# A decay table with the head innermost, and its rows from a second set of powers

## The chip, the cores and the metric

The kernel runs on one NeuronCore of one Trainium2 chip. Five engines work beside each other: TensorE (PE, with its weight loads as PEld), VectorE (DVE), ScalarE (ACT), GpSimd (POOL) and SyncE (SP), which only issues DMAs. The metric is the time of one execution in microseconds (us), as the median of several runs. Before the change it is 601.41 us, the median of 3 runs from 600.75 to 603.45.

## What is computed

Three layers follow each other. The first is retention attention over 2 batches, 8 heads, 768 positions and 64 columns per head, with one decay factor per head:

```
Dmask = where(i >= j, lam[h] ** (i - j), 0)            # within a block
intra = ((q @ k.T) * Dmask) @ v
inter = (q * lam[h] ** (i + 1)) @ kv_state             # from the blocks before
out   = intra + inter
kv_state = lam[h] ** block * kv_state + (k * lam[h] ** (block - 1 - j)).T @ v
```

Its output, 1536 tokens by 512, goes through `relu(x @ w_in)**2 @ w_out` (2048 hidden columns) and then through `(sigmoid(x @ w_gate) * (x @ w_val)) @ w_out` (1536 hidden columns). All is float32. The decay factors `lam` are an input, so the tables of their powers are made on the chip.

## The kernel before

The attention works in chunks of 128 positions (CH), so there are 12 chunks, 6 for each batch, taken in the order ORDER. Two tables hold the decay. `D` is [128, 8, 128]: for each key position j (the partition; keys lie in reverse order), head h and query position i, it holds lam to the power that the pair needs, or zero. `L` is [128, 4, 128]: lam to the power i + 1 for the head to which the partition belongs.

`powers()` (L203) makes them. It loads `lam` into `lam_sb`, POOL raises it to powers 1 to 128 (`W`, L217), and ACT's queue stores 127 zeros, a one and these powers as one row of 256 numbers per head in DRAM (`w_dram`, L216 and L219). `decays()` (L223) reads them back: for D each partition starts one element further on in every head's row, so it reads eight pieces of 512 bytes, one for each head. L is read in pieces of 512 bytes too, four per partition (L231).

A chunk takes these steps. `att_scores` (L258) is q times k on PE, with two heads side by side. `att_prep` (L269) has POOL make `kd`, which is k times the last column of D (L278), and `qd`, q times L (L285), while DVE makes `at`, scores times D (L287), in two instructions per chunk, one for the even heads and one for the odd. `att_decay` (L293) is `tt` on POOL, `att_out` (L301) the products with v and with the state, `att_state` and `att_x` the evacuations. POOL does nothing after the attention.

The first 7 chunks (LEAD) are a prologue. It starts with the loads: FIRST and SIDE name q/k and k/v loads that precede D and L, EARLY (L28) those that follow: "D v1 w q4" is the two tables, the second k/v, a weight and the fifth q/k. The q's of SIDE go through ACT's queue, all others through SP's. The 5 other chunks lie in the first 16 steps of the first layer (`step_1`), which PE fills with matrix products. Beside them ACT and DVE turn weights into the form that PE uses: DVE's `m`, `u` and `wlo` (L172 to L167, L374) belong to that. Each engine works through its instructions in the order in which the program issues them; nothing overtakes.

After the 16 steps, `strassen` computes the rest of the first layer with fewer products (`block`, L545, after `combine_x` and `combine_a`), then come `pair_out` (L695) and the second layer in the same three stages.

Of the kernel before, what the change touches and what calls it, by code (L numbers as in the profile page):

```python
# [7 lines left out]
F32 = mybir.dt.float32  # L8
F32R = mybir.dt.float32r
AF = mybir.ActivationFunctionType  # L10
ALU = mybir.AluOpType

P = 128
CH = 128
# [10 lines left out]

FIRST = "q0 q1 v0"
SIDE = "q2 q3"
EARLY = "D v1 w q4"  # L28
LOOP = ("v2 v3 q5", "q6 v4 v5 w", "v6 w v7", "q7", "", "", "")
RAW_BUFS = 4  # L30

# [9 lines left out]
def retention_moe_kernel(  # L41
# [24 lines left out]
    nc = tc.nc  # L66
# [3 lines left out]
    H = lam.shape[0]  # L70
    NF1 = w1.shape[0]
    NF2 = w2.shape[0]
    I32 = mybir.dt.int32

    const = ctx.enter_context(tc.tile_pool(name="const", bufs=1))
    dram = ctx.enter_context(tc.tile_pool(name="dram", bufs=1, space=bass.MemoryType.DRAM))
# [5 lines left out]
    def bank():  # L82
        return ps.tile([P, 512], F32, tag="p", name="p")

    def unit(name, dt=F32):
        return up.tile([P, 512], dt, tag="u", name=name)

    def double(name, dt=F32):
        return wp.tile([P, 2, 512], dt, tag="w", name=name)
# [21 lines left out]
    def load_qk(c, eng=nc.sync):  # L111
        qk_t[c] = double("qk")
        eng.dma_start(out=qk_t[c], in_=qk[c].rearrange("a t p b -> a t (p b)"))

    def load_kv(c, eng=nc.sync):
        kv_t[c] = double("kv")
        eng.dma_start(out=kv_t[c], in_=kv[c].rearrange("s t h d -> s t (h d)"))
# [12 lines left out]
    def load_w(n):  # L130
        for _ in range(min(n, len(to_load))):
            ph, f, u = key = to_load.pop(0)
            t = wp.tile([P, 512, 2], I32, tag="w", name="raw")
            src = (w1 if ph == 1 else w2)[f, u].bitcast(I32)
            nc.sync.dma_start(out=t, in_=src.rearrange("p (n two) -> p n two", two=2))
            raw_t[key] = t
# [51 lines left out]
    def run(ops):  # L188
        weave(ops, [])


    lam_sb = const.tile([P, 1], F32, name="lam_sb")
    exi = const.tile([P, 8], I32, name="exi")
    ex = const.tile([P, 8], F32, name="ex")
    W = const.tile([P, 8], F32, name="W")
    Z = const.tile([H, 128], F32, name="Z")
    warm = const.tile([P, P], mybir.dt.bfloat16, name="warm")
    D = const.tile([P, H, CH], F32, name="D")
    L = const.tile([P, 4, CH], F32, name="L")
    S = [const.tile([P, 4, 64], F32, name=f"S{i}", tag=f"S{i}") for i in range(2)]  # L200
    w_dram = dram.tile([H, 256], F32, name="w_dram")

    def powers():  # L203


        src = bass.AP(lam.tensor, lam.offset, [[1, H], [0, 16], [1, 1]])
        nc.sync.dma_start(out=lam_sb, in_=src)
        nc.vector.memset(warm, 0.0)
        nc.gpsimd.iota(exi, pattern=[[1, 8]], base=0, channel_multiplier=8)
        nc.vector.memset(Z[:, 0:127], 0.0)  # L210
        nc.vector.memset(Z[:, 127:128], 1.0)
        nc.vector.tensor_scalar(
            out=exi, in0=exi, scalar1=127, scalar2=None, op0=ALU.bitwise_and
        )
        nc.vector.tensor_scalar(out=ex, in0=exi, scalar1=1.0, scalar2=None, op0=ALU.add)
        nc.scalar.dma_start(out=w_dram[:, 0:128], in_=Z)  # L216
        nc.gpsimd.tensor_tensor(out=W, in0=lam_sb.to_broadcast([P, 8]), in1=ex, op=ALU.pow)  # L217
        dst = w_dram[:]
        nc.scalar.dma_start(  # L219
            out=bass.AP(dst.tensor, dst.offset + 128, [[256, H], [8, 16], [1, 8]]), in_=W  # L220
        )

    def decays():  # L223


        src = w_dram[:]
        nc.sync.dma_start(
            out=D, in_=bass.AP(src.tensor, src.offset, [[1, P], [256, H], [1, CH]])
        )
        for r in range(2):  # L230
            nc.sync.dma_start(  # L231
                out=L[64 * r : 64 * r + 64],
                in_=bass.AP(src.tensor, src.offset + 256 * r + 128, [[0, 64], [512, 4], [1, CH]]),
            )

    def warm_up():

        t = bank()
        for _ in range(WARM):
            nc.tensor.matmul(t[:, 0:P], lhsT=warm, rhs=warm, start=True, stop=True)  # L240

    Dv = D.rearrange("j (p r) i -> j r p i", r=2)

# [9 lines left out]
    def pv(t):  # L255
        return t.rearrange("a (p b) -> a p b", p=4)
# [12 lines left out]
    def att_prep(c):  # L269
        n = c % SEQ_CH  # L270
        sc = sc_t.pop(c)
        at_t[c] = double("at")
        dst = [pv(at_t[c][:, r, :]) for r in range(2)]
        qt = qk_t.pop(c)[:, 0, :]
        kn = kv_t[c][:, 0, :]
        if n < SEQ_CH - 1:
            kd = kd_t[c] = unit("kd")
            nc.gpsimd.tensor_tensor(  # L278
                out=kd.rearrange("s (h d) -> s h d", h=H),
                in0=kn.rearrange("s (h d) -> s h d", h=H),  # L280
                in1=D[:, :, CH - 1 : CH].to_broadcast([P, H, 64]), op=ALU.mult,
            )
        if n > 0:
            qd = qd_t[c] = unit("qd")
            nc.gpsimd.tensor_tensor(out=pv(qd), in0=pv(qt), in1=L, op=ALU.mult)  # L285
        return [
            lambda r=r: nc.vector.tensor_tensor(  # L287
                out=dst[r], in0=pv(sc[r]), in1=Dv[:, r], op=ALU.mult
            )
            for r in range(2)  # L290
        ]
# [431 lines left out]
    def load(what, eng=nc.sync):  # L723

        for x in what.split():
            if x == "w":
                load_w(1)
            elif x == "D":
                decays()
            elif x[0] == "q":  # L730
                load_qk(order[int(x[1:])], eng)
            else:
                load_kv(order[int(x[1:])], eng)
# [4 lines left out]
    for k in range(lead, NCH):  # L738
        a, b = SLOTS[k - lead]
# [64 lines left out]

    with tc.manual_schedule():
        powers()
        load(FIRST)
        load(SIDE, nc.scalar)
        warm_up()
        load(EARLY)  # L810
        new_xr()
        for k in range(UP):
            att_scores(order[k])
        run(att_prep(order[0]))
        for k, c in enumerate(order[:lead]):
            att_out(c)
            if UP <= k + 3 < lead:
                att_scores(order[k + 3])
            load(LOOP[k])
            ops = conv_dve()  # L820
            if k + 1 < lead:
                weave(att_prep(order[k + 1]), ops[:2])
                run(att_state(c))
                att_decay(order[k + 1])
                weave(ops[2:], att_x(c))
            else:
                weave(split_w(1, 0), ops)
                rest.append(c)
            for m in range(CONVS[k]):
                if m:  # L830
                    run(conv_dve())
                conv_act()
            flush()


        keys = [(1, i, 0) for i in range(NF1 // 2)]
        prepare_a(keys[0], T1)
        at(T1 - 20.0, lambda: load_a((1, 1, 0)))
        combine_x([T1 + d for d in (-30, -25, -15, -13, -11, -9, -7, 2, 4, 6, 8)])
        for f in range(NF1):  # L840
            step_1(f)
        n_out = 24
        for k in range(n_out):
            convert(T2 + 1.0 + k * (T3 - T2 - 4.0) / n_out)
        for f in range(NF1):
            prepare_out(1, f, T2 + 24 * MM * f)
        uses = [use for i in range(NF1 // 2) for use in pair_in_1(i)]
        strassen(keys, uses, (None, lambda: close(1)))
        xc.clear()
        new_xr()  # L850
        for f in range(2):
            at(T3 - 24.0 + f, lambda f=f: load_units(2, f))
        at(T3 - 14.0, lambda: run(split_w(2, 0)))
        pair_out(1)


        for f in range(2, NF2):
            at(T3 + (36 * (f - 1) - 12) * MM - 8.0, lambda f=f: load_units(2, f))
        for k in range(3 * NF2 - n_out):
            convert(T3 + 2.0 + 3.6 * k)  # L860
        keys = [(2, i, u) for i in range(NF2 // 2) for u in range(2)]
        prepare_a(keys[0], T4)
        at(T4 - 20.0, lambda: load_a((2, 0, 1)))
        combine_x([T4 - 46.0 + 3.5 * k for k in range(11)])
        for f in range(NF2):
            step_2(f)
        for f in range(NF2):
            prepare_out(2, f, T5 + 24 * MM * f)
        uses = [use for i in range(NF2 // 2) for use in pair_in_2(i)]
        strassen(keys, uses, (None, lambda: close(2)))  # L870
        pair_out(2)
        flush()
        assert not agenda and not to_conv and not ready
# [7 lines left out]
def _layout(q, k, v, lam, moe_w_in, moe_w_out, moe2_w_gate, moe2_w_val, moe2_w_out):  # L881
    import numpy as np

    B, H, S, D = q.shape
    n = S // CH
# [50 lines left out]
```

## Time and profile before

| | |
|---|---|
| median of 3 runs | 601.41 us |
| the profiled execution: its own time | 601.51 us |
| its span (first to last instruction) | 599.4 us |
| PE busy | 582.6 us, 97% |
| DVE busy | 448.6 us, 75% |
| ACT busy | 332.5 us, 55% |
| POOL busy | 36.9 us, 6% |

The profile names instructions by line, engine and operation, with what they write and read (`at<-p,D` writes tile at from p and D). Times count from the start of the span. The span is 2.1 us shorter than the execution's own time, which takes in what lies around it. PE is busy in nearly all of the span, but its share says nothing of the first 45 us, where it waits for the tables, nor of the places in which another engine sets the pace. Those are read from windows of time, from the list of waits and from the chain of work that ended last.

### The profile page before, as it was taken

The numbers are of one execution on the slowest core, as the hardware profiler recorded it, in microseconds if no ns is written. First come the engines' busy times: TensorE is split into PE (matmuls) and PEld (weight loads), VectorE is DVE, ScalarE is ACT, GpSimd is POOL, SyncE is SP. The second block draws the span as 40 slices with busy tenths as digits, with TensorE's granted clock in tenths as the row PEclk, the third lists the DMA queues.
The fourth block names the chain that finished last, engine by engine and source line by source line (L and its number), as shares of the span: only waits on it lengthen the run. The fifth ranks groups of instructions, "written<-read, shape, count | busy, mean of one in ns | idle before, by whom it ended". The sixth has DMA issues, their size and how long they took to land.

```text
span 599.4 us, 8496 instructions
## 1 busy us (share of the span) xinstructions
PE 582.6 (97%) x3076; PEld 478.8 (80%) x3076; DVE 448.6 (75%) x673; ACT 332.5 (55%) x525; POOL 36.9 (6%) x34
## 2 busy tenths in 40 slices
PE   7799999999899999999999999999999999999997
PEld 7677878887678888888888888888888888888885
DVE  0699998999888868988877788694778787569101
ACT  0367787988556456756557654554464455537101
POOL 1672212100000000000000000000000000000000
PEclk9899999999999999999999999999999999999999
DMA  7996898682145377999978945511332422658003
GB/s 212 402 418 232 306 309 331 237 297 87 57 121 208 107 240 271 408 414 415 410 276 279 312 170 172 163 50 54 122 106 106 140 81 80 209 187 357 0 1 141
DMA packets 53578, 127.19 MB, mean 212 GB/s; under 512 B 5784, under 2 KB 7584, under 8 KB 53536
## 3 DMA queue, kind: packets, MB, share of 16 engines
q1 hardware_dynamic: 52376, 124.41, 57.9%
q10 hardware_dynamic: 1160, 2.24, 1.1%
q8 instruction: 24, 0.39, 0.3%
q14 instruction: 18, 0.15, 0.1%
HBM read 90.96 MB, written 35.66 MB: 211 GB/s over the span
## 4 chain that ended last, share of the span: by engine, by line
PE 87%; DVE 4%; DMA 2%; POOL 2%; issue 2%; ACT 1%; SPq 0%; ACTq 0%; POOLq 0%; DVEq 0%
PE p L545 30%; PE p L695 25%; PE p L386 17%; PE p L400 12%; DMA kv<-in_kv 1%; POOL kd L278 1%; PE p L329 1%; PE p L322 1%; POOL qd L285 1%; DMA lam_sb<-in_lam 1%; PE p L264 1%; DVE wlo L374 1%; DVE al L526 1%; DVE m L175 1%; ACT ah L520 1%
## 5 line engine op out<-in xcount | busy, mean ns | idle before, releaser
L545 PE MATMUL p<-xcl,ah 128*128 128x512 f32 x280 | 109.1, 390 | 2.5 <-DVE xcl L469 2.5
L545 PE MATMUL p<-xch,ah 128*128 128x512 f32 x280 | 109.4, 391 | 0.4 <-ACT s L554 0.2
L545 PE MATMUL p<-xch,al 128*128 128x512 f32 x280 | 109.0, 389 | 0.0
L695 PE MATMUL p<-g2h,whi 128*128 128x512 f32 x224 | 87.1, 389 | 0.0
L695 PE MATMUL p<-g2l,whi 128*128 128x512 f32 x224 | 87.1, 389 | 0.0
L695 PE MATMUL p<-g2h,wlo 128*128 128x512 f32 x224 | 87.1, 389 | 0.0
L545 PEld LDWEIGHTS p<-xcl,ah 128*128 128x128 f32 x280 | 52.6, 188 | 13.5 <-DVE xcl L469 2.9
L545 PEld LDWEIGHTS p<-xch,ah 128*128 128x128 f32 x280 | 52.5, 188 | 12.9 <-ACT s L554 1.4
L545 PEld LDWEIGHTS p<-xch,al 128*128 128x128 f32 x280 | 52.6, 188 | 11.0
L559 DVE TENSOR_TENSOR c<-p,s 128x512 f32<-128x512 f32 x60 | 41.2, 688 | 25.3 <-PE p L545 21.4
L554 ACT COPY s<-p 128x512 f32<-128x512 f32 x60 | 35.0, 586 | 37.4 <-PE p L545 37.4
L167 DVE CUSTOM_DVE_ANT_0 u<-m,r 128x1024 uint16<-128x1024 uint16 x68 | 49.5, 728 | 2.7
L374 DVE TENSOR_TENSOR wlo<-u,whi 128x512 fp32r<-128x512 f32 x68 | 46.1, 707 | 7.0 <-ACT whi L372 5.7
L150 ACT ACTIVATE j<-raw 128x512 f32<-128x512 f32 x68 | 45.6, 671 | 10.2 <-issue 5.3
L175 DVE SCALAR_TENSOR_TENSOR m<-j,m 128x512 int32<-128x512 int32 x68 | 49.5, 728 | 1.2
L151 ACT ACTIVATE r<-raw 128x512 int32<-128x512 uint32 x68 | 45.2, 665 | 8.7 <-PE p L695 5.5
L695 PEld LDWEIGHTS p<-g2l,whi 128*128 128x128 f32 x224 | 42.0, 188 | 8.8
L695 PEld LDWEIGHTS p<-g2h,whi 128*128 128x128 f32 x224 | 42.0, 188 | 8.7
L695 PEld LDWEIGHTS p<-g2h,wlo 128*128 128x128 f32 x224 | 42.0, 188 | 8.7
L372 ACT CAST whi<-u 128x512 fp32r<-128x512 f32 x68 | 39.0, 616 | 13.7 <-DVE u L167 13.2
L386 PE MATMUL p<-xh,wlo 128*128 128x512 f32 x160 | 43.2, 392 | 1.1 <-DVE wlo L374 1.1
L386 PE MATMUL p<-xh,whi 128*128 128x512 f32 x160 | 43.8, 395 | 0.0
(87 smaller groups left out, 911.6 us busy)
## 6 DMA issues: line engine op xcount, KB each, us to landing
raw<-in_w SPq DMA_DIRECT2D x68, 512.0 KB, 7.1
w<-u SPq DMA_DIRECT2D x68, 256.0 KB, 4.0
u<-w SPq DMA_DIRECT2D x64, 256.0 KB, 5.5
g<-g SPq DMA_DIRECT2D x56, 256.0 KB, 4.4
g<-g SPq DMA_DIRECT2D x28, 512.0 KB, 7.5
a<-w SPq DMA_DIRECT2D x20, 512.0 KB, 4.3
kv<-in_kv SPq DMA_DIRECT2D x12, 512.0 KB, 8.6
qk<-in_qk SPq DMA_DIRECT2D x10, 512.0 KB, 5.7
```

The lines of the kernel that those rows point to most:

```text
L150: nc.scalar.activation(j, t[:, :, 1].bitcast(F32), AF.Copy, scale=2.0**-112)
L151: nc.scalar.activation(r, t[:, :, 0].bitcast(mybir.dt.uint32), AF.Copy, scale=2.0**-29)
L167: nc.vector.tensor_tensor(out=w.bitcast(I32), in0=m, in1=r, op=ALU.add)
L175: lambda: nc.vector.scalar_tensor_tensor(out=m, in0=j, scalar=-(2**31), in1=m, op0=ALU.bitwise_and, op1=ALU.bitwise_or),
L372: nc.scalar.copy(hi, src)
L374: lambda lo=lo, src=src, hi=hi: nc.vector.tensor_tensor(out=lo, in0=src, in1=hi, op=ALU.subtract)
L386: nc.tensor.matmul(acc, lhsT=a[:, kk * P : (kk + 1) * P], rhs=b[:, kk, :], start=i == 0, stop=i == 11,)
L400: nc.tensor.matmul(acc[e], lhsT=a[:, e * P : (e + 1) * P], rhs=b, start=first and i == 0, stop=last and i == 2,)
L545: nc.tensor.matmul(acc, lhsT=w[:, col, kk * P : (kk + 1) * P], rhs=x[:, kk, :], start=start and i == 0, stop=stop and i == 5, skip_group_c ...
L554: nc.scalar.copy(s, acc)
L559: nc.vector.tensor_tensor(out=c, in0=acc, in1=s, op=ALU.add)
L695: nc.tensor.matmul(acc[e, t], lhsT=a[:, e * P : (e + 1) * P], rhs=b[:, t, :], start=first and i == 0, stop=last and i == 2,)
```

## The change

D becomes [128, 128, 8]: query position first, head innermost. In DRAM the 256 rows of `d_dram` hold 8 numbers each, one per head, and a partition reads 1024 numbers in a row, one piece of 4 KB. The powers for it, `W_h`, come from a load of `lam` that gives each partition all 8 factors. `at` reads D through `Dv` with the head innermost, so two numbers that follow each other for it lie 8 elements (32 bytes) apart.

L no longer comes from the same rows. POOL computes a second set of powers, `W_r`, from two further loads of `lam` on ACT's queue; it is stored behind the loads of SIDE (`store_rows`) and read back in pieces of 2 KB (`load_rows`) behind the fifth q ("L" at the end of EARLY).

```diff
-EARLY = "D v1 w q4"
+EARLY = "D v1 w q4 L"
...
-    D = const.tile([P, H, CH], F32, name="D")
+    D = const.tile([P, CH, H], F32, name="D")
...
-        src = bass.AP(lam.tensor, lam.offset, [[1, H], [0, 16], [1, 1]])
-        nc.sync.dma_start(out=lam_sb, in_=src)
+        nc.sync.dma_start(out=lam_h, in_=bass.AP(lam.tensor, lam.offset, [[0, P], [1, H]]))
         nc.vector.memset(warm, 0.0)
-        nc.gpsimd.iota(exi, pattern=[[1, 8]], base=0, channel_multiplier=8)
-        nc.vector.memset(Z[:, 0:127], 0.0)
-        nc.vector.memset(Z[:, 127:128], 1.0)
+        nc.gpsimd.iota(ei_h, pattern=[[1, 1]], base=1, channel_multiplier=1)
+        nc.gpsimd.iota(ei_r, pattern=[[1, 8]], base=0, channel_multiplier=8)
+        nc.vector.tensor_copy(e_h, ei_h)
+        nc.vector.memset(Z[:, 0 : 127 * H], 0.0)
+        nc.vector.memset(Z[:, 127 * H :], 1.0)
+        nc.scalar.dma_start(out=d_dram[0:128].rearrange("(o t) h -> o (t h)", o=1), in_=Z)
+        for r in range(2):
+            nc.scalar.dma_start(
+                out=lam_r[64 * r : 64 * r + 64],
+                in_=bass.AP(lam.tensor, lam.offset + r, [[2, 4], [0, 16], [1, 1]]),
+            )
+        nc.gpsimd.tensor_tensor(out=W_h, in0=lam_h, in1=e_h.to_broadcast([P, H]), op=ALU.pow)
+        nc.scalar.dma_start(out=d_dram[128:256], in_=W_h)
...
+        nc.gpsimd.tensor_tensor(out=W_r, in0=lam_r.to_broadcast([P, 8]), in1=e_r, op=ALU.pow)
+
+    def store_rows():
         nc.scalar.dma_start(
-            out=bass.AP(dst.tensor, dst.offset + 128, [[256, H], [8, 16], [1, 8]]), in_=W
+            out=l_dram.rearrange("r (q b) -> (r q) b", b=8), in_=W_r
         )
 
     def decays():
-        src = w_dram[:]
+        src = d_dram[:]
         nc.sync.dma_start(
-            out=D, in_=bass.AP(src.tensor, src.offset, [[1, P], [256, H], [1, CH]])
+            out=D.rearrange("j i h -> j (i h)"),
+            in_=bass.AP(src.tensor, src.offset, [[H, P], [1, CH * H]]),
         )
+
+    def load_rows():
+        src = l_dram[:]
         for r in range(2):
             nc.sync.dma_start(
-                out=L[64 * r : 64 * r + 64],
-                in_=bass.AP(src.tensor, src.offset + 256 * r + 128, [[0, 64], [512, 4], [1, CH]]),
+                out=L[64 * r : 64 * r + 64].rearrange("a p i -> a (p i)"),
+                in_=bass.AP(src.tensor, src.offset + 4 * CH * r, [[0, 64], [1, 4 * CH]]),
             )
...
-    Dv = D.rearrange("j (p r) i -> j r p i", r=2)
+    Dv = D.rearrange("j i (p r) -> j r p i", r=2)
...
-                in1=D[:, :, CH - 1 : CH].to_broadcast([P, H, 64]), op=ALU.mult,
+                in1=D[:, CH - 1, :].unsqueeze(2).to_broadcast([P, H, 64]), op=ALU.mult,
...
         load(SIDE, nc.scalar)
+        store_rows()
         warm_up()
```

On SP's queue, at the program's start, the two loads of L stand before the change right behind the load of D, and the second k/v (`kv`), the first weight (`raw`) and the fifth q/k (`qk`) follow.

```order
L207 DMA lam_sb<-in_lam 128x1x1
L113 DMA qk<-in_qk 128x1024 x2
L117 DMA kv<-in_kv 128x1024
L227 DMA D<-w_dram 128x8x128
L231 DMA L<-w_dram 64x4x128 x2
L117 DMA kv<-in_kv 128x1024
L135 DMA raw<-in_w 128x1024
L113 DMA qk<-in_qk 128x1024
L117 DMA kv<-in_kv 128x1024 x2
```

On the same queue after the change the loads of L have moved behind that q/k, ahead of the next two k/v.

```order
L211 DMA lam_h<-in_lam 128x8
L113 DMA qk<-in_qk 128x1024 x2
L117 DMA kv<-in_kv 128x1024
L240 DMA D<-d_dram 128x1024
L117 DMA kv<-in_kv 128x1024
L135 DMA raw<-in_w 128x1024
L113 DMA qk<-in_qk 128x1024
L249 DMA L<-l_dram 64x512 x2
L117 DMA kv<-in_kv 128x1024 x2
```

All that moved on SP is the pair of L loads, past three loads of 512 KB each; the program makes them wait for the store of `W_r`. On ACT, the start of the program after the change holds three more DMA issues: the two small loads of `lam` (`lam_r`), and the store of `W_r` between the two q/k loads and the table load.

```order
L218 DMA d_dram<-Z 1x1024
L220 DMA lam_r<-in_lam 64x1x1 x2
L225 DMA d_dram<-W_h 128x8
L113 DMA qk<-in_qk 128x1024 x2
L233 DMA l_dram<-W_r 128x8
L360 ACT_TABLE_LOAD
```

Behind these rows ACT's order is as it was, and PE's is unchanged throughout. DVE's and POOL's differ only ahead of the first `at` and the first `kd`, in the few instructions that make the powers.

## Rows read from the trace of the kernel before

**Rows 1.** The page: span, busy time and share of two engines.
```profile
PE 582.6 (97%) x3076; PEld 478.8 (80%) x3076; DVE 448.6 (75%) x673; ACT 332.5 (55%) x525; POOL 36.9 (6%) x34
```
**Rows 2.** Waits, 0 to 45 us: who waited for whom, total, times, longest.
```profile
DVE at L287 <- DMA D<-w_dram: 14.8, 1, 14.8
...
POOL kd L278 <- DMA D<-w_dram: 9.1, 1, 9.1
...
POOL kd L278 <- DMA kv<-in_kv: 4.7, 2, 2.6
POOL W L217 <- DMA lam_sb<-in_lam: 4.4, 1, 4.4
```
**Rows 3.** The chain, 0 to 70 us: start, length, what.
```profile
0.74 4.49 DMA lam_sb<-in_lam
...
5.37 1.65 POOL W L217
...
7.04 2.35 DMA w_dram<-W
...
19.27 1.06 POOL kd L278
...
22.95 1.54 POOL kd L278
24.49 1.69 POOL qd L285
```
**Rows 4.** Windows: length, busy time (instructions) by engine, PEclk, DMA share, GB/s.
```profile
9.00:10.00 1.00, 1.00 (x14) 1.00 (x12) 0.00 (x0) 0.73 (x1) 0.00 (x0) 1.00 0.79 147
...
12.00:13.00 1.00, 0.96 (x16) 0.96 (x16) 0.00 (x0) 0.00 (x0) 0.00 (x0) 1.00 1.03 183
13.00:14.00 1.00, 0.78 (x10) 0.58 (x9) 0.00 (x0) 0.00 (x0) 0.00 (x0) 0.85 0.79 231
14.00:15.00 1.00, 1.00 (x13) 1.00 (x10) 0.00 (x0) 0.00 (x0) 0.00 (x0) 0.50 1.05 297
15.00:16.00 1.00, 0.30 (x4) 0.00 (x1) 0.00 (x0) 0.00 (x0) 0.00 (x0) 0.50 1.27 341
...
17.00:30.00 13.00, 11.08 (x179) 9.48 (x181) 9.43 (x16) 4.69 (x9) 8.31 (x9) 0.86 1.02 415
```
**Rows 5.** Longer windows: length, then PE, PEld, DVE, ACT, POOL, as before.
```profile
16.10:20.00 3.90, 2.74 (x32) 2.43 (x32) 2.48 (x4) 0.37 (x1) 1.78 (x2) 0.50 1.01 379
20.00:30.00 10.00, 8.34 (x149) 7.04 (x149) 7.78 (x13) 4.32 (x8) 7.38 (x8) 0.97 1.02 417
30.00:45.00 15.00, 13.93 (x192) 10.89 (x192) 14.96 (x23) 9.23 (x17) 11.93 (x10) 1.00 1.03 418
...
55.00:135.00 80.00, 80.00 (x511) 64.54 (x510) 75.46 (x125) 66.58 (x115) 10.96 (x8) 1.00 0.84 294
...
155.00:167.00 12.00, 9.30 (x39) 6.73 (x37) 11.59 (x16) 5.53 (x8) 0.00 (x0) 1.00 0.25 87
```
**Rows 6.** Groups of DVE's instructions: busy us, mean ns, idle time before.
```profile
L287 DVE TENSOR_TENSOR at<-p,D 128x512 f32<-128x512 f32 x24 | 15.6, 679 | 14.8 <-DMA D<-w_dram 14.8
...
L344 DVE TENSOR_TENSOR S<-p,tt 128x256 f32<-128x256 f32 x8 | 3.3, 416 | 1.3 <-PE p L329 1.2
...
L210 DVE MEMSET Z<- 8x127 f32 x1 | 0.2, 164 | 0.0
```
**Rows 7.** The same view, of ACT.
```profile
L150 ACT ACTIVATE j<-raw 128x512 f32<-128x512 f32 x68 | 45.6, 671 | 10.2 <-issue 5.3 <-PE p L695 2.4 <-PE p L386 1.1
...
L651 ACT ACTIVATE r<-c 128x512 f32<-128x512 f32 x18 | 11.4, 632 | 17.7 <-DVE c L559 16.2 <-DMA g<-g 1.6
```
**Rows 8.** Timeline, 0 to 24 us: start, length, what.
```profile
9.49 0.39 SPq L227 DMA_DIRECT2D D<-w_dram  x1
...
11.37 0.62 SPq L117 DMA_DIRECT2D kv<-in_kv  x1
12.04 0.83 SPq L135 DMA_DIRECT2D raw<-in_w  x1
12.91 0.66 SPq L113 DMA_DIRECT2D qk<-in_qk  x1
```

More of the change, by code (lines that the diff above doesn't have):

```diff
@@ L189, in run @@
         weave(ops, [])
[L192 to L196, printed above, removed]
+    lam_h = const.tile([P, H], F32, name="lam_h")
+    ei_h = const.tile([P, 1], I32, name="ei_h")
+    e_h = const.tile([P, 1], F32, name="e_h")
+    W_h = const.tile([P, H], F32, name="W_h")
+    Z = const.tile([1, 128 * H], F32, name="Z")
@@ L197, in retention_moe_kernel @@
+    lam_r = const.tile([P, 1], F32, name="lam_r")
+    ei_r = const.tile([P, 8], I32, name="ei_r")
+    e_r = const.tile([P, 8], F32, name="e_r")
+    W_r = const.tile([P, 8], F32, name="W_r")
     warm = const.tile([P, P], mybir.dt.bfloat16, name="warm")
-    D = const.tile([P, H, CH], F32, name="D")
+    D = const.tile([P, CH, H], F32, name="D")
     L = const.tile([P, 4, CH], F32, name="L")
     S = [const.tile([P, 4, 64], F32, name=f"S{i}", tag=f"S{i}") for i in range(2)]
-    w_dram = dram.tile([H, 256], F32, name="w_dram")
+    d_dram = dram.tile([256, H], F32, name="d_dram")
@@ L203, in powers @@
+    l_dram = dram.tile([2, 4 * CH], F32, name="l_dram")
     def powers():
-        src = bass.AP(lam.tensor, lam.offset, [[1, H], [0, 16], [1, 1]])
-        nc.sync.dma_start(out=lam_sb, in_=src)
+        nc.sync.dma_start(out=lam_h, in_=bass.AP(lam.tensor, lam.offset, [[0, P], [1, H]]))
         nc.vector.memset(warm, 0.0)
-        nc.gpsimd.iota(exi, pattern=[[1, 8]], base=0, channel_multiplier=8)
-        nc.vector.memset(Z[:, 0:127], 0.0)
-        nc.vector.memset(Z[:, 127:128], 1.0)
+        nc.gpsimd.iota(ei_h, pattern=[[1, 1]], base=1, channel_multiplier=1)
[11 more added lines that the diff above has]
+        nc.scalar.dma_start(out=d_dram[128:256], in_=W_h)
@@ L212, in powers @@
         nc.vector.tensor_scalar(
-            out=exi, in0=exi, scalar1=127, scalar2=None, op0=ALU.bitwise_and
+            out=ei_r, in0=ei_r, scalar1=127, scalar2=None, op0=ALU.bitwise_and
         )
[L215 to L218, printed above, removed]
+        nc.vector.tensor_scalar(out=e_r, in0=ei_r, scalar1=1.0, scalar2=None, op0=ALU.add)
@@ L729, in load @@
                 decays()
+            elif x == "L":
+                load_rows()
             elif x[0] == "q":
```

## The prediction

> **What bounds the kernel now.** I read the page's busy shares first [rows 1]. PE is busy 97% of the span, so the time moves only where PE waits, or where it starts its long run of products later or earlier. The change touches tables that are made in the first 16 us and used until about 120 us, so I went on to that part. The list of waits [rows 2] shows DVE idle for 14.8 us and POOL for 9.1 us until D lands, and POOL for 4.7 us more until k/v loads land. The chain [rows 3] tells the same in order: lam takes 4.49 us to land, the powers 1.65, their store 2.35, then come D and the k/v loads, then POOL's kd and qd without a pause from 22.95 on. What the reader is to see there is that the third kd, at 22.95, starts when its k/v load is in: the DMA queue sets that moment.
>
> Then the windows by microsecond [rows 4]. From 17 to 30 us the DMA engines move 415 GB/s. From 12 to 16, where D and L pass in pieces of 512 bytes, it is 183, 231, 297 and 341, at a busy share near 1.
>
> Last the longer windows [rows 5], for DVE. From 16.1 to 20 it is busy 2.48 of 3.9 us, from 20 to 30 it is 7.78 of 10, and from 30 to 45 it is 14.96 of 15: the second half of the prologue is DVE's. From 55 to 135 PE is busy all 80 us and DVE 75.46, so DVE has 4.54 us to spare. From 155 to 167 PE is busy 9.30 of 12 and DVE 11.59.
>
> **The change part by part.** *D and L in longer pieces.* Windows 12 to 16 moved 183 + 231 + 297 + 341 = 1052 KB in 4 us; at 415 GB/s that is 2.5 us, so 1.5 us are to be had. D is issued at 9.49 [rows 8] and the rate has its low at 12 to 13, so a part of the loss is a late start of the many pieces; if D starts earlier still, it takes another 0.6 us of the second in which only 147 GB/s were moved (9 to 10). I take 1.8 us, between 1.5 and 2.1. The lower bound of the term is 0, if the start and not the size of the pieces costs the time and does not move. D lands that much sooner, the second k/v sooner by the passage of L too, and the third k/v, which sets POOL's run, by the 1.8 us.
>
> *The load of lam.* It reads 32 bytes per partition now, for 4 bytes before. Nearest rows: the load before, 4.49 us, and the small store, 2.35 [rows 3]. I take no change, and keep 2.1 us sooner as the other end. Later than before has no row that speaks for it.
>
> *Zeros and powers.* The memset of Z has 1016 numbers on one partition where 127 took 164 ns [rows 6]; in proportion that is at most 1.3 us. It delays the store of Z, which has until the powers are stored at 9.4 us. The second pow on POOL costs another 1.65 us; POOL waits for D anyway. That cover is gone only if the new loads of lam land after about 12.3 us, since the first kd stands behind W_r in POOL's order. Issued behind Z's store, near 3 to 4 us, they would have to take twice the 4.49 us. Cost 0, other end about 1 us.
>
> *The wait of L.* Before the loads of L, SP now waits for the store of W_r, and behind them stand two k/v loads, a q/k and the weights. SP issues D, k/v, raw and q/k in 0.39 + 0.62 + 0.83 + 0.66 = 2.5 us [rows 8], so it comes to L at about 12 us. W_r is ready near 9, its store goes out when the SIDE loads are issued, about 10, and takes 2.35 or, behind their data, some 2 us more: SP may stand for 0.4 to 2.4 us. The queue then holds four loads of 512 KB, 5 us at 415 GB/s, and that covers it. Without that cover it costs what is left of the wait on the third k/v, one to one.
>
> *The read of D by `at`.* This is the term that decides. Nothing moves in DVE's order, but each of the 24 `at` takes its second operand in steps of 32 bytes instead of a row. An `at` takes 679 ns with 512 elements per partition, an instruction of the same kind with 256 takes 416 [rows 6]: 1.03 ns for an element, 0.15 us fixed. No row of DVE has such a read. Lower bound: no cost. Nearest row with a step: ACT reads raw in steps of 8 bytes in 671 ns, and a row without steps in 632 [rows 7], 39 ns more, though with another function. Upper bound: each element costs a second pass, 512 times 1.03 = 0.53 us. I take the upper bound. In the ACT row two numbers still stand within 16 bytes and the step shows all the same; at 32 bytes each number stands alone, four times as far apart.
>
> [...] No row of this case shows a step of 32 bytes on DVE. [...]
>
> *The sum.* 16 of the 24 `at` run before 55 us, 14 in the prologue and 2 in the first steps: 16 x 0.53 = 8.5 us more on an engine that has no idle time from 30 to 45. Of the 1.42 us that DVE is idle between 16.1 and 20 I let half, 0.7, take some of it up; the 2.22 us from 20 to 30 are waits for POOL and PE, which move with their releasers. The other 8 `at` cost 4.2 us, and the 4.54 us of idle time from 55 to 135 hide them. D and the loads give 1.8 back. 8.5 - 0.7 - 1.8 = +6.0 us on 601.5 of the profiled execution, 607.5. That execution is 0.1 us over the median of the runs, so 607.4 us. With all idle time before 30 us used up, 3.64 us, and 2.1 back, it is +2.8; with none used and nothing back +8.5.
>
> **The rivals.** *The step costs DVE nothing.* Then only the DMA term is left: -1.8 us, 599.6 us, not slower. It speaks for it that PE's and POOL's waits at the start all end with D and the loads behind it, and that DVE's 0.15 us of fixed time and one element per nanosecond look like a limit of its own pace rather than of a read. Against it stands the ACT row. The end of the run moves with the third kd, as DVE has 3.64 us of idle time before 30 us and can follow.
>
> *The step costs half.* ACT's 39 ns are for one element skipped; for the seven that `at` skips, in proportion, 0.27 us. 16 x 0.27 = 4.4, less 0.7 to 3.6 of idle time and 1.8 of DMA: between -1.0 and +1.9, 601.9 us in the middle. The term passes the gain at (1.8 + 0.7) / 16 = 0.16 us per `at`, and 3 us of loss at 0.34.
>
> *The start moves too.* If lam lands 2.1 us sooner, D is stored and issued sooner and meets idle DMA engines, and with a free step the gain is 1.8 + 1.7 = 3.5, 597.9 us. The q loads, which begin behind lam's on SP's queue, would have to move too, and no row says that they wait for it.
>
> *The wait of L bites.* SP stands until past 17 us; the two k/v loads behind L are then late by what is over. With a free step and 2 us lost it is 601.6, no change. Against it: by its parts above the store has landed by 14.4 us.
>
> **How the numbers follow.** Strided read at its full price, 607.4 us: 0.50. Half price, 601.9: 0.13. Free, 599.6: 0.25. Free with an earlier start, 597.9: 0.08. Free or half with the wait of L or no gain of DMA, about 601.6: 0.04. 0.5% is 3.0 us, about what a measurement of this kernel can tell from no change. Slower by more takes 0.47 of the first case (its low end, +2.8, is just inside 0.5%) and 0.03 of the half price, 0.50. Faster by more takes the early start and 0.03 of the free read, whose DMA term may be larger, 0.11. The rest is 0.39. The first case alone runs from 604.2 to 609.9; with the cases of the other sign the range is 598.6 to 608.8.
>
> **What would show it.** The mean of the 24 `at`: about 1.2 us by the forecast, 0.68 by the rival, 0.95 at half price; nothing else decides as much. The windows from 12 to 16 us should show over 400 GB/s, D's release of the first kd near 14.3 for 16.1, the third kd near 21 for 22.95. L's loads should not hold the k/v behind them: POOL's third kd must not wait longer than before. With the forecast, DVE's busy share from 20 to 30 us rises to nearly all, PE's first L386 starts 1 to 2 us later than before or not sooner, and from 55 to 135 PE stays full. A mean of `at` under 0.9 us makes the prediction wrong, and so does a DVE that takes the added time in its idle stretches before 30 us.

## The result, and the profile after

The changed kernel takes 609.69 us (median of 6 runs, 608.53 to 612.59); the kernel before, beside it, 601.53 (6 runs). The ratio is 1.0127, 95% interval 1.0106 to 1.0148: slower by 1.3%, 0.9 us above the end of the predicted range. The profiled execution takes 610.21 us with a span of 608.1, 8.7 more than before.

Busy times on the page, as in [rows 1]:

```profile
PE 586.0 (96%) x3076; PEld 481.0 (79%) x3076; DVE 461.9 (76%) x674; ACT 332.4 (55%) x525; POOL 36.9 (6%) x36
```

DVE has 13.3 us more work and ACT and POOL have none. Its groups (lines have moved, `at` is now L305), as in [rows 6]:

```profile
L305 DVE TENSOR_TENSOR at<-p,D 128x512 f32<-128x512 f32 x24 | 25.7, 1106 | 12.5 <-DMA D<-d_dram 12.5
...
L216 DVE MEMSET Z<- 1x1016 f32 x1 | 0.9, 905 | 0.1
```

An `at` takes 1106 ns where it took 679: the step of 32 bytes costs 0.43 us, not nothing and not 0.53. The large memset takes 0.9 us and delays nobody.

The chain of 0 to 60 us, for [rows 3]: start, length, what.

```profile
0.74 2.84 DMA lam_h<-in_lam
...
3.72 1.65 POOL W_h L224
...
5.39 2.99 DMA d_dram<-W_h
...
8.47 0.33 SPq L240
...
8.84 7.33 DMA kv<-in_kv
...
16.24 1.04 POOL kd L296
...
23.45 1.04 POOL kd L296
24.50 1.71 POOL qd L303
```

`lam` lands 1.65 us sooner and D is issued at 8.47, 1.0 us sooner. All the same the third `kd` starts at 23.45, later than the 22.95 of before. SP's waits, 0 to 45 us (who waited for whom, total, times, longest), and the timeline say why:

```profile
SPq L249 <- DMA l_dram<-W_r: 7.3, 1, 7.3
SPq L240 <- DMA d_dram<-W_h: 5.8, 1, 5.8
```

```profile
10.03 0.33 ACTq L233 DMA_DIRECT2D l_dram<-W_r  x1
...
17.63 1.14 SPq L249 DMA_DIRECT2D L<-l_dram  x2
18.81 1.06 SPq L117 DMA_DIRECT2D kv<-in_kv  x2
```

SP stands at L's loads for 7.3 us, until 17.6, because the 4 KB store of `W_r`, issued at 10.03, lands only then. D, the second k/v, the weight and the fifth q/k were all issued on the other queue before it: D lands at 14.9, the k/v at 16.2, and the rate falls from 412 GB/s (15 to 16 us) to 263 and 111 (16 to 17 and 17 to 18). The two k/v loads behind L are issued at 18.8, and from 17 to 20 us the DMA engines have little to move. The windows show it, and the rest of the way (length; PE, PEld, DVE, ACT, POOL; granted clock; DMA share; GB/s), for [rows 4, 5]:

```profile
12.00:16.00 4.00, 1.65 (x26) 1.26 (x22) 1.01 (x2) 0.00 (x0) 1.04 (x1) 1.00 1.02 369
17.00:20.00 3.00, 2.83 (x32) 2.64 (x32) 2.29 (x4) 1.11 (x3) 0.28 (x1) 0.51 0.30 111
20.00:30.00 10.00, 7.50 (x130) 6.43 (x132) 9.33 (x13) 3.45 (x7) 6.14 (x6) 0.98 1.01 379
30.00:45.00 15.00, 12.11 (x177) 10.08 (x176) 15.00 (x20) 7.32 (x13) 10.45 (x9) 0.89 1.03 409
37.50:41.00 3.50, 3.26 (x28) 2.94 (x30) 3.50 (x5) 0.00 (x0) 3.37 (x3) 0.51 1.03 410
55.00:135.00 80.00, 79.64 (x542) 63.76 (x542) 77.52 (x119) 63.45 (x111) 10.80 (x8) 1.00 0.76 272
150.20:153.60 3.40, 3.40 (x10) 2.63 (x9) 3.39 (x4) 1.95 (x4) 0.00 (x0) 0.50 0.08 30
```

The DMA part of the change works: 369 GB/s from 12 to 16 us (over 400 was expected), where [rows 4] have 263 in the mean. It is lost again at 111 GB/s from 17 to 20. DVE is busier from 20 to 30 (9.33 for 7.78 us), full from 30 to 45, and has 2.48 us of idle time left from 55 to 135 (4.54 before). Three rows show a granted clock near 0.5 of full (0.51, 0.51 and 0.50). Each stretch follows a wait of PE, of 2.42 us up to 16.17, of 1.60 up to 37.74 and of 2.08 up to 149.03.

The first product of the 16 steps (`xh`) and the first product of `block`, after and then before:

```profile
44.81 1.20 PE L404 MATMUL p<-xh,whi 128*128 128x512 f32 x4
...
155.33 0.40 PE L563 MATMUL p<-xch,ah 128*128 128x512 f32 x1
```

```profile
41.42 1.20 PE L386 MATMUL p<-xh,whi 128*128 128x512 f32 x4
...
147.25 0.39 PE L545 MATMUL p<-xch,ah 128*128 128x512 f32 x1
```

So 3.4 us are lost up to the steps, 4.7 in them, and 0.6 in all the rest. A part of the loss in the steps is seen in PE's waits from 45 us on, after and then before:

```profile
PE p L404 <- DVE wlo L392: 3.1, 4, 2.1
PE p L563 <- DVE xcl L487: 2.4, 1, 2.4
```

```profile
PE p L545 <- DVE xcl L469: 2.5, 1, 2.5
PE p L386 <- DVE wlo L374: 1.1, 2, 0.7
```

PE waits 2.0 us more for `wlo`, and its longest single wait is 2.1 us for 0.7. PE's timeline around that wait (groups of four products; in brackets the idle time ahead):

```profile
142.92 1.09 PE L418 MATMUL p<-gh,whi 128*128 128x512 f32 x4
...
149.03 1.20 PE L404 MATMUL p<-xh,wlo 128*128 128x512 f32 x4 [2.08 <-DVE wlo L392]
150.06 1.80 PE L404 MATMUL p<-xl,whi 128*128 128x512 f32 x4
151.66 1.91 PE L418 MATMUL p<-gh,whi 128*128 128x512 f32 x4
```

Behind the wait four products take 1.8 to 1.9 us for 1.09. The 3.4 us at half the clock lose another 1.7. Waits and clock together are 3.7 of the 4.7 us. The clock does not always fall here: in before_step32, below, it stays full (1.00) behind the same wait.

### The profile page after: what moved, and what is told of

The parts are those of the page before. It is cut to its first block, busy times and chain, and to the rows that moved or that the text cites. A ratio compares the mean times of both kernels' runs of the same rounds, so it can differ in the third digit from the quotient of the medians.

```text
span 608.1 us, 8504 instructions
## 1 busy us (share of the span) xinstructions
PE 586.0 (96%) x3076; PEld 481.0 (79%) x3076; DVE 461.9 (76%) x674; ACT 332.4 (55%) x525; POOL 36.9 (6%) x36
## 4 chain that ended last, share of the span: by engine, by line
PE 79%; DVE 12%; issue 3%; DMA 3%; ACT 2%; POOL 1%; ACTq 0%; SPq 0%; DVEq 0%; POOLq 0%
PE p L563 31%; PE p L713 25%; PE p L404 13%; PE p L418 8%; DVE at L305 2%; DVE m L175 2%; DVE u L167 2%; DVE wlo L392 1%; DVE m L172 1%; DMA kv<-in_kv 1%; DVE xcl L487 1%; DVE gl L447 1%; DVE t L498 1%; PE p L347 1%; DMA d_dram<-W_h 0%
## 5 line engine op out<-in xcount | busy, mean ns | idle before, releaser
L563 PEld LDWEIGHTS p<-xcl,ah 128*128 128x128 f32 x280 | 52.9, 189 | 13.8 <-DVE xcl L487 2.9
L167 DVE CUSTOM_DVE_ANT_0 u<-m,r 128x1024 uint16<-128x1024 uint16 x68 | 53.1, 781 | 2.7
```

Source lines behind the costliest of these rows:

```text
L167: nc.vector.tensor_tensor(out=w.bitcast(I32), in0=m, in1=r, op=ALU.add)
L563: nc.tensor.matmul(acc, lhsT=w[:, col, kk * P : (kk + 1) * P], rhs=x[:, kk, :], start=start and i == 0, stop=stop and i == 5, skip_group_c ...
```

## Experiments

Ratios are to the kernel before on the same chip, with 95% intervals; 1% is 6.0 us. "Step" is the distance in D between two numbers that `at` reads in succession.

### The step and the place of L, in two by two

**before_step32**: the kernel before, with the step alone.

```diff
-    Dv = D.rearrange("j (p r) i -> j r p i", r=2)
+    Dv = D.rearrange("j h i -> j (h i)").rearrange("j (i p r) -> j r p i", p=4, r=2)
```

> The kernel before, with its loads and its tables as they were; only the view through which at reads D is changed, to steps of 32 bytes (so it multiplies by the wrong entries of D, and the output is not the reference's). Theory (the step itself costs about 0.42 us per at, on an engine that sets the pace from 30 to 45 us): the mean of at 1.09 us for 0.68, time 606 to 608 us. Rival (DVE's idle time takes the longer at up, and the loss of the change lies in the loads): the same mean of at, time within 2 us of the kernel before, 601 to 603.5.

Measured: 609.6 us, 1.0124 [1.0089, 1.0159], `at` 1109 ns. The step by itself makes a loss as large as the whole change's, and a larger one than was expected. PE's longest wait for `wlo`, which ends at 148.42, and the window behind it:

```profile
PE p L386 <- DVE wlo L374: 3.1, 4, 2.1
```

```profile
149.10:152.50 3.40, 3.40 (x17) 2.81 (x16) 3.40 (x4) 2.65 (x6) 0.00 (x0) 1.00 0.33 126
```

The wait is that of the changed kernel, but here the clock stays full. The steps, from 44.17 to 153.09, are 3.1 us longer than before and not 4.7: the difference, 1.6 us, is about what the half clock was put at.

**after_row_read**: the changed kernel with `at` reading rows again.

```diff
-    Dv = D.rearrange("j i (p r) -> j r p i", r=2)
+    Dv = D.rearrange("j i h -> j (i h)").rearrange("j (p r i) -> j r p i", p=4, r=2)
```

> The changed kernel, with all its loads and stores; only at reads D as a row without steps (wrong entries, so the output is not the reference's). Theory (two costs: the step, and the store of W_r that holds SP for 7.3 us and makes the third k/v late): mean of at 0.68 us, the third kd still near 23.4 us, time 601.5 to 604 us, no gain over the kernel before. Rival (the step is the whole loss, the hold of SP is covered): 599 to 600.5 us.

**after_L_late**: the changed kernel with L's loads behind the two k/v loads.

```diff
-EARLY = "D v1 w q4 L"
-LOOP = ("v2 v3 q5", "q6 v4 v5 w", "v6 w v7", "q7", "", "", "")
+EARLY = "D v1 w q4"
+LOOP = ("v2 v3 L q5", "q6 v4 v5 w", "v6 w v7", "q7", "", "", "")
```

> The changed kernel with the two loads of L moved behind the third and fourth k/v, so that these are not held behind the store of W_r. Theory (two costs): the third kd at 19 to 21 us for 23.45, time 604 to 606.5 us, 3 to 5 us under the changed kernel. Rival (DVE sets the end of the prologue with its long at, so an earlier k/v is given back): 608 to 610 us.

**after_row_L_late**: both edits.

> Both edits: at reads D as a row (wrong entries, so the output is not the reference's) and the loads of L stand behind the third and fourth k/v. Theory (two costs, which add up): 597.5 to 599.5 us, 2 to 4 us under the kernel before, which is what the earlier loads are worth. Rival (the earlier loads are worth nothing): 601 to 602 us.

| | us | ratio | third `kd` at |
|---|---|---|---|
| changed kernel | 609.69 | 1.0127 [1.0106, 1.0148] | 23.45 |
| after_row_read | 603.07 | 1.0009 [0.9989, 1.0029] | 21.91 |
| after_L_late | 607.48 | 1.0096 [1.0067, 1.0125] | 21.42 |
| after_row_L_late | 601.06 | 0.9975 [0.996, 0.9991] | 20.50 |

The step costs 1.2% with L in either place (1.0127 to 1.0009, 1.0096 to 0.9975). L's wait costs 0.3%, 2 us. With the row read that is clear of the noise, with the step it is not: the intervals of 1.0127 and 1.0096 overlap. Three expectations missed: after_row_read's third `kd` comes at 21.91 and not near 23.4, and the two versions with L late gain less than the theory had. What is left of the DMA's gain without both is 0.25%, 1.5 us, though the third `kd` comes 2.45 us sooner.

### What a step costs

**step_map**: the kernel before, with another step in each pair of chunks.

```diff
+STEPS = (1, 2, 3, 4, 5, 8, 1, 2, 3, 4, 5, 8)
...
+            [list(D.ap[0]), [{2: 256, 3: 128, 4: 128, 8: 2, 5: 64}[step], 4], [step, CH]],
```

> The kernel before, where at reads D in steps of 1, 2, 3, 4, 5 and 8 elements (4 to 32 bytes), four instructions of each in the prologue and the first steps (wrong entries of D, so the output is not the reference's). Theory (a number that shares its 16 bytes with no neighbour costs more): 0.68 us for 1 and 2, about 1.1 for 4 and over, 3 between them. Rival (the cost grows with the step): 0.68, 0.74, 0.80, 0.86, 0.92, 1.1 us.

DVE's groups, one line for each step (L297: 4 bytes, L299: 8, L301: 12, L303: 16, L305: 20, L306: 32):

```profile
L305 DVE TENSOR_TENSOR at<-p,D 128x512 f32<-128x512 f32 x4 | 4.3, 1109 | 0.0
L306 DVE TENSOR_TENSOR at<-p,D 128x512 f32<-128x512 f32 x4 | 4.3, 1103 | 0.0
L303 DVE TENSOR_TENSOR at<-p,D 128x512 f32<-128x512 f32 x4 | 4.1, 1073 | 0.0
...
L301 DVE TENSOR_TENSOR at<-p,D 128x512 f32<-128x512 f32 x4 | 3.3, 840 | 0.0
...
L297 DVE TENSOR_TENSOR at<-p,D 128x512 f32<-128x512 f32 x4 | 2.6, 682 | 14.8 <-DMA D<-w_dram 14.8
L299 DVE TENSOR_TENSOR at<-p,D 128x512 f32<-128x512 f32 x4 | 2.6, 681 | 0.0
```

8 bytes are free, 12 cost 0.16 us, 16 cost 0.39, and 20 and 32 little more (0.42 to 0.43). In the changed kernel the price also differs with the place, 0.39 us in the prologue and 0.47 in the steps, so the last three are not told apart. In these rows the price goes with how many numbers stand in 16 bytes and not with the length of the step: two at a step of 8 bytes (681 ns), four in 48 bytes at 12 (840), one at most from 16 on (1073 to 1109, and 32 bytes take no longer than 20). What makes it so, no run shows.

### Where the added time is lost

**pro_step32** and **late_step32**: the kernel before, with the step only in the 14 `at` of the prologue, or only in the 10 of the steps (`>=` in place of `<`).

`Ds` is D read in steps of 32 bytes, as in before_step32.

```diff
...
+        table = Ds if order.index(c) < LEAD else Dv
...
```

> The kernel before with steps of 32 bytes in the 14 at of the prologue alone (wrong entries, so the output is not the reference's): 14 x 0.42 = 5.9 us more on DVE. Theory (DVE sets the pace in the prologue, and what it is late by there it does not make up): 4 to 6 us over the kernel before. Rival (DVE's idle time from 55 to 135 us takes it up): 0 to 2 us.

> The kernel before with steps of 32 bytes in the 10 at of the first steps alone (wrong entries, so the output is not the reference's): 10 x 0.42 = 4.2 us more on DVE. The prediction's claim (the idle time of 55 to 135 us hides the last 8): at most 1 us over the kernel before. Rival (that idle time lies in waits which stay, so the last step's wlo and the first block's operands are late by most of it): 2 to 4 us over.

Measured: 605.43 us, 1.0048 [1.0026, 1.0071] for the 14 (+2.9 us), and 607.84 us, 1.010 [1.0065, 1.0135] for the 10 (+6.0 us). Both expectations missed, in opposite directions. The 14 add 5.6 us to DVE (14 x 0.40, 1078 ns for 678) and half of it shows. The 10 add 4.6 (10 x 0.46, 1137 ns for 680), most of which was taken to be hidden, and all of it shows: the interval is 3.9 to 8.1 us. A wait of PE, and then a window, of late_step32:

```profile
PE p L388 <- DVE wlo L376: 3.1, 4, 2.1
```

```profile
148.30:151.70 3.40, 3.40 (x10) 2.65 (x9) 3.40 (x4) 1.57 (x4) 0.00 (x0) 0.50 0.33 129
```

These are the changed kernel's wait and its stretch at half the clock, without any change in the prologue.

**step32_7_8** and **step32_10_11**: the step in two chunks alone, near 52 and 68 us, or near 104 and 122 (`order.index(c) in (7, 8)` or `(10, 11)`).

> The kernel before with steps of 32 bytes in 4 at alone, those of the eighth and ninth chunk, near 52 and 68 us (wrong entries, so the output is not the reference's): 4 x 0.46 = 1.8 us more on DVE. Theory (DVE's idle time of 55 to 135 us lies from 65 to 95 us, behind these two, and takes them up): 0 to 0.8 us over the kernel before. Rival (no idle time of DVE's in the steps is of use): 1.5 to 3 us over.

> The kernel before with steps of 32 bytes in 4 at alone, those of the last two chunks, near 104 and 122 us (wrong entries, so the output is not the reference's): the same 1.8 us more on DVE. Theory (little idle time is left behind them, and the last step's wlo and the first block's operands wait for DVE): 1.5 to 4 us over the kernel before, with PE's wait near 145 us at 2 us for 0.66. Rival (the place doesn't matter): as the run with the eighth and ninth chunk.

Measured: 603.39 us, 1.0022 [1.0004, 1.004], for the early pair, +1.3 us; 605.09 us, 1.0049 [1.0034, 1.0064], for the late pair, +2.9 us, with the same 1.8 us added to DVE. PE's longest wait for `wlo`, in the early pair and then in the late one:

```profile
PE p L388 <- DVE wlo L376: 1.8, 3, 1.1
```

```profile
PE p L388 <- DVE wlo L376: 2.4, 2, 2.1
```

The early pair lies between the theory and its rival. So the place counts, though the two intervals overlap slightly. In the late pair's profile slow products follow the wait (four take 2.05 us, the next four 1.84 and the four behind them 1.08), as at half the clock in the changed kernel; in the early pair's there are none (1.20 and 1.07). They may be a part of the larger loss. Windows of the kernel before show what the row from 55 to 135 hid:

```profile
75.00:85.00 10.00, 10.00 (x56) 8.09 (x55) 9.07 (x16) 8.61 (x16) 1.58 (x1) 1.00 0.98 317
85.00:95.00 10.00, 10.00 (x68) 8.03 (x67) 8.23 (x15) 8.25 (x16) 1.15 (x2) 1.00 0.90 331
...
105.00:115.00 10.00, 10.00 (x81) 8.11 (x81) 9.04 (x15) 8.82 (x17) 1.59 (x1) 1.00 0.70 262
115.00:125.00 10.00, 10.00 (x56) 8.05 (x56) 9.78 (x17) 8.88 (x15) 0.00 (x0) 1.00 0.69 233
125.00:135.00 10.00, 10.00 (x68) 8.03 (x67) 9.97 (x19) 9.37 (x16) 0.00 (x0) 1.00 0.90 311
```

2.70 of the 4.54 us of idle time lie from 75 to 95, 1.18 from 105 to 125, and 0.03 from 125 to 135. Idle time at 85 us cannot take up an `at` at 104 or 122. What is not taken up behind these reaches the `wlo` for which PE waits longest.

### Why L's store is late

**L_behind_D**: the changed kernel with `EARLY = "D L v1 w q4"`.

> The changed kernel with the loads of L right behind that of D on SP's queue. Theory (the store of W_r lands only after the bulk loads that were issued before it, on whichever queue): with only D and the two q/k of SIDE ahead of it, the store lands near 13.5 to 14.5 us for 17.6. Rival (the store itself takes 7 us): still 17 to 18 us.

Measured: 610.28 us, one run. SP's wait, and then its timeline:

```profile
SPq L249 <- DMA l_dram<-W_r: 5.1, 1, 5.1
```

```profile
13.86 1.15 SPq L249 DMA_DIRECT2D L<-l_dram  x2
```

With only D issued ahead of it on SP's queue, the store lands at 13.8, and with three more loads ahead at 17.6. In lamr_first, next, D and one k/v are ahead of it, and it lands at 16.3. In these three runs it lands the later, the more loads are issued ahead of it on the other queue.

**lamr_first**: the changed kernel with the two loads of `lam_r` ahead of Z's store on ACT, so that `W_r` might be stored sooner.

> The changed kernel with the two loads of lam for W_r first on ACT's queue, ahead of the store of Z. Theory: they land near 5 us for 8.2, W_r is ready near 7 us and stored ahead of D's load, and the store lands by 12.5 us; SP stands for under 2.5 us at L for 7.3, the third kd starts at 19 to 21 us for 23.45, and the time is 2 us under the changed kernel, about 1.0% over the kernel before. Rival (the loads for W_r delay lam_h and so D): no better than the changed kernel, 1.3% over.

Measured: 609.02 us, 1.0112 [1.0079, 1.0145]. Mostly a miss: `lam_r` still lands near 8.4, SP stands 4.9 us for 7.3, D is issued at 9.67 for 8.47, and the third `kd` starts at 23.71.

### Versions that might win

**laid_out**: D is loaded as in the changed kernel into a spare tile; ACT copies it into rows, and `at` and `kd` read those. L late.

```diff
...
+        nc.scalar.copy(last_col, raw[:, (CH - 1) * H :])
+        for r in range(2):
+            nc.scalar.copy(D[:, r], raw.rearrange("j (i p r) -> j r p i", p=4, r=2)[:, r])
...
```

> The changed kernel with L behind the fourth k/v, and with D read by steps only once: ACT, idle until then, copies it into two tables whose rows at reads without steps, and its last column for kd. Theory: at 0.68 us, the first at about 1 us after D has landed, and DVE makes that up; 600 to 602.5 us against 602.9 for the kernel before, 0 to 2.5 us faster. Rival (the copies on ACT delay the start of the chain one to one): 602.5 to 604.5.

Measured: 601.87 us, 0.9997 [0.9976, 1.0018]. All of the step's loss is gone, and no gain of the DMA is measured.

**pairs_L_late**: D with two heads innermost (a step of 8 bytes, pieces of 1 KB), L late. **pairs_lamr**: the same with `lam_r` first and L behind the fifth q.

```diff
...
+    D = const.tile([P, 4, CH, 2], F32, name="D")
+    d_dram = dram.tile([4, 256, 2], F32, name="d_dram")
...
+            out=d_dram[:, 128:256].rearrange("p t r -> t p r"),
...
```

> The changed kernel with L behind the fourth k/v, and with D as four tables of two heads each, [128, 4, 128, 2], in pieces of 1 KB: at reads it in steps of 8 bytes. Theory (8 bytes are free, as the map of steps shows): at 0.68 us, and the time of the row read with L late, 0.2 to 0.3% under the kernel before. Rival (the pieces of 1 KB, and the powers stored in pieces of 8 bytes, give the gain back): 0 to 0.3% over.

> D as four tables of two heads each, and the loads of lam for W_r first on ACT's queue, L behind the fifth q as in the changed kernel. Theory (both costs of the change are gone and its earlier loads are left): at 0.68 us, third kd at 19 to 21 us, 0.2 to 0.5% under the kernel before. Rival (DVE sets the end of the prologue, earlier loads are worth nothing): within 0.1% of it.

Measured: 604.39 us, 1.0029 [1.0011, 1.0046], and 603.71 us, 1.0027 [1.0013, 1.0042]. Neither has the gain that the theory gave it. `at` is at 681 ns, but the powers are now stored in pieces of 8 bytes, and D is issued at 11.86 and 12.04 for 8.47. SP's wait in the first:

```profile
SPq L246 <- DMA d_dram<-W_h: 9.2, 1, 9.2
```

**lam16**: the kernel before with `lam` read in the order [16, 8] for [8, 16], and L late, from the same table.

```diff
...
-        src = bass.AP(lam.tensor, lam.offset, [[1, H], [0, 16], [1, 1]])
+        src = bass.AP(lam.tensor, lam.offset, [[0, 16], [1, H], [1, 1]])
...
```

> The kernel before, with D as it was and read as a row, and with two things of the change that cost nothing: lam is loaded in a pattern whose slowest dimension is 16 instead of 8, and L stands behind the fourth k/v, without a second set of powers. Theory (an earlier D and an earlier third k/v move the end of the prologue): lam lands near 3.5 us for 5.2, D's issue at 8.4 for 9.5, the third kd near 21.5 for 22.95, the time 0.5 to 1.5 us under the kernel before. Rival (DVE sets the end of the prologue): no change.

Measured: 602.06 us, 0.9997 [0.9982, 1.0011]. `lam` lands at 3.97 for 5.23, the third `kd` starts at 21.71 for 22.95, and the time does not move: earlier loads alone are worth little. The first `xh` product starts at 41.87 us for 41.42. That DVE sets the second half of the prologue [rows 5] is the likely reason; no run isolates it.

## Why the prediction was right or wrong

The direction and the main cause were right: the step of `at`. The sum, +6.0, came 2 us short of the measured +8.2 (by the medians; 7.6 by the ratio), with errors in both directions.

- *D in longer pieces, -1.8 us.* The loads were faster, as said: 369 GB/s from 12 to 16 us for 263. D lands at 14.9 for 16.1, and after_row_L_late has the third `kd` 2.45 us sooner, with the sooner `lam` in it. The time gains 1.5 us there, and lam16 gains nothing from 1.2 us at the same place: the term holds roughly, but a load that is sooner does not count one to one.
- *lam, no change.* It landed 1.65 us sooner, near the other end that was kept (2.1). The memset and the second power cost nothing, as said.
- *The wait of L, hidden.* This step failed. The store was taken to land by 14.4 us; it landed at 17.6. It was priced by its own size and the two q loads ahead of it on ACT's queue, and not by the four loads on SP's. The rival "SP stands until past 17 us" is what happened, only together with a paid step. It costs 2.0 us and takes back all of the DMA's gain: -1.8 became +0.5 on the third `kd` in the profiled execution (in after_row_read, with the same loads, the store lands at 16.3 and the third `kd` is 1.0 us sooner than before).
- *The price of the step.* 0.53 us was taken and 0.43 measured (0.39 in the prologue, 0.47 in the steps): the step is paid, as said, and the size was a fifth too large, 10.2 us over the 24 `at` for 12.7. The 0.53 us was an estimate, a second pass for each element at 1.03 ns; no row of before had such a read, and no run shows a second pass.
- *Where it is paid.* This is the step that failed most: "The other 8 `at` cost 4.2 us, and the 4.54 us of idle time from 55 to 135 hide them." The 10 `at` of the steps (these 8 and two near 53 us), measured alone, cost 6.0 us; the last 4 alone cost 2.9, and the prologue's 14, which were to carry the loss, also 2.9. The idle time was added up over 80 us, and much of it lies ahead of the last `at`. The sum also had no term for TensorE's clock. In the profile of the changed kernel 3.4 us at half the clock follow PE's wait and cost 1.7 us; in that of before_step32 the clock stays full behind the same wait.

The two parts measured alone add up to 8.9 us, but before_step32 with both loses 7.5 by its ratio, and the profile puts 3.4 of the whole loss ahead of the steps. That the prologue's `at` cost less than they add stays open. So does what the half clock from 37.5 to 41 us costs, and so does 1.0 of the 4.7 us lost in the steps. A part of that 1.0 may lie beside POOL, below, which no run isolates. The start of the first `xh` product also differs between kernels with an unchanged prologue, 41.4 to 43.5 us in single profiles, so a split to a tenth of a microsecond isn't to be had from these.

## What to carry to other kernels

A layout that makes a load faster can be paid for by the instructions that read it: on VectorE a step of 8 bytes is free here (681 ns for 682), and one of 16 or more makes the instruction 1.6 times as long (1073 to 1109 ns). Idle time covers added work only where it lies behind that work and ahead of the next wait (the same 1.8 us of DVE cost 1.3 us near 52 and 68 us, 2.9 us near 104 and 122), so read it in short windows and follow the work to whom it is late for. Here a store of 4 KB that is waited for landed at 13.8, 16.3 and 17.6 us with one, two and four large loads, from D on, issued ahead of it on another queue, so put its reader far enough back or its store ahead of them.

## What the runs showed of the hardware

- The same wait of PE of 2.1 us for `wlo`, ending between 145 and 149 us, is followed by half the clock in some profiles and not in others. In the changed kernel and in late_step32, 3.4 us at a granted clock of 0.50 follow, and four products take up to 1.91 us; in step32_10_11 they take 2.05 and 1.84. In before_step32 (a granted clock of 1.00) and in after_L_late the first four take 1.20 and 1.21 and those behind them 1.07 to 1.09. What decides is not shown. Waits of 0.7 us (the kernel before) and 1.1 us (step32_7_8) at this place are followed by 1.20 and then 1.07 to 1.08, too.
- Many of DVE's instructions are longer beside POOL's. In the changed kernel POOL works from 63.09 to 66.87 us; DVE's timeline there:

```profile
62.81 0.68 DVE L392 TENSOR_TENSOR wlo<-u,whi 128x512 fp32r<-128x512 f32 x1
63.42 1.53 DVE L167 CUSTOM_DVE_ANT_0 u<-m,r 128x1024 uint16<-128x1024 uint16 x1
64.87 1.51 DVE L172 TENSOR_SCALAR m<-j 128x512 int32<-128x512 int32 x1
66.31 1.10 DVE L447 TENSOR_TENSOR gl<-g,gh 128x512 fp32r<-128x512 f32 x1
```

`u` takes 0.69 us elsewhere and `m` 0.42 (the whole group of `u` grows from 49.5 to 53.1 us). Over the four stretches from 55 to 125 us in which POOL works, DVE's instructions are longer by about 6.8 us after and 5.6 before, worked out against those two, and 0.68 for the others. The longer `at` moves other instructions beside POOL's, which may add 1.2 us to its price. Why they are longer there, no run shows.
- Stored in pieces of 8 bytes, the 4 KB of powers land 3.4 us later than in pieces of 32 bytes: SP waits 9.2 us for them in pairs_L_late and 5.8 in the changed kernel (D issued at 11.86 for 8.47).
